# Five more dummy matmuls at the start of a TensorE-bound kernel

## The chip, the cores and the metric

One core of one Trainium2 chip. The metric is device microseconds per execution, the median of several runs; less is better. Each run also lists its span (first to last instruction that the profile shows) and the mean granted clock of TensorE.

## The reference

One transformer block, bfloat16: 2048 rows of 512, modulated layer norm, attention of 32 query heads on 8 key/value heads over the last 512 positions, output projection, then a second modulated layer norm and a ReLU MLP of width 1792.

```
mod = (silu(c) @ w_mod).reshape(1, 6, 1, -1)          # sa, ca, ga, sb, cb, gb
h = layernorm(x) * (1 + ca) + sa
x = x + ga * attention(h, k_cache, v_cache, wq, wo)   # last 512 keys, 32 heads of 128
h = layernorm(x) * (1 + cb) + sb
x = x + gb * (relu(h @ w1) @ w2)
```

## The kernel before

A dummy is a 128x512 product of ones that nobody reads:

```python
def warm(n, gate=(), bk=7):
    for i in range(n):
        mm(bank[bk], ones[:, :], ones[:, 0:1].to_broadcast([P, QB]), True, True, [R_ones] + list(gate), [bk], i == n - 1)
...
    warm(10)                      # from 1.1 us on, while x loads
...
    ln_stat(0)
    warm(3, [R_mv[0]])            # "gated" dummies: behind the statistics of a row tile
    ln_stat(1)
    warm(2, [R_mv[1]])
...
    fs = mod_cols_mm(0, QBK)      # 32 products of one column, in 4 chunks of 8;
    for f in fs:                  # each chunk waits for its own transfer of w_mod
        f()
    ln_tposes(0, TB[0])           # 4 transposes of 128x128
    mod_cols_evac(0, QBK)         # VectorE
...
    ln_tposes(1, TB[0])
    warm(2, bk=1)                 # "the pair"
    ln_norm(2)
    mod_half(0, 0, DVE)           # h = norm * (1 + ca) + sa, from PSUM
    mod_half(0, 2, ACT)
    ln_tposes(2, TB[1])
    ln_tposes(3, TB[1])
    mod_half(0, 1, DVE)
    mod_half(0, 3, ACT)
    q_half(0, 0, CC_ORDER, QBK)   # first query products
```

## Time and profile before

| | before |
|---|---|
| time, median | 560.38 us (560.31 to 560.55) |
| span of the profiled execution | 559.0 us, of 560.87 |
| time beyond the span | 1.9 us |
| TensorE busy | 553.9 us (99%) |

TensorE is the bound from 11.65 us on without a hole (about 0.35 us over the median distances of its shapes in 547 us). The columns are: stretch and length; busy time of TensorE, weight loads, VectorE, ScalarE, GpSimd; mean granted clock; DMA share and GB/s. Before:

```profile
555.00:558.90 3.90, 0.80 (x15) 0.62 (x12) 1.23 (x5) 0.00 (x0) 0.00 (x0) 1.00 0.26 71
558.90:561.00 2.10, 0.00 (x0) 0.00 (x0) 0.00 (x0) 0.00 (x0) 0.00 (x0) 0.72 0.04 12
561.00:564.00 3.00, 0.00 (x0) 0.00 (x0) 0.00 (x0) 0.00 (x0) 0.00 (x0) 0.97 0.00 0
```

No instruction is shown behind 559.0, yet the clock column goes on: the clock's records here say half clock (0.50, from 559.83 us on), and time without a record counts as full (the column reads 1.00 from 0 us on, though the dummies up to 6.56 us start 0.43 us apart and the later ones 0.22). 0.97 over 3 us therefore means that the records stop at about 561.2 (exactly: at 561.17). The execution goes on for some 2 us behind the span.

### The profile page before, as it was taken

The page shows a single profiled execution, that of the slowest core. Times are in us where ns is not written, and L with a number is a line of the kernel's source. Part 1 is how long each engine was busy: PE and PEld are TensorE (multiplying, and loading weights), DVE is VectorE, ACT ScalarE, POOL GpSimd, SP SyncE. Part 2 cuts the span into 40 slices and gives each one's busy share as a digit, 9 for nine tenths or more (in the row PEclk, how much of TensorE's full clock was granted, in tenths as well). Part 3 has the DMA queues.
Part 4 walks back from the last instruction along what each step waited for, and adds up shares of the span by engine and source line. Part 5 has one row for each costly group of instructions (what it writes and reads, how often), then busy time and mean ns, then how long its engine had stood idle before and what let it go on. Part 6 is the DMA issues. An engine that isn't in the chain of part 4 may idle for free.

```text
span 559.0 us, 9759 instructions
## 1 busy us (share of the span) xinstructions
PE 553.9 (99%) x4139; PEld 316.6 (57%) x4139; DVE 254.9 (46%) x556; ACT 349.4 (63%) x455; POOL 52.7 (9%) x50
## 2 busy tenths in 40 slices
PE   8999999999999999999999999999999999999997
PEld 4665555555555555555555555555555554444444
DVE  5555555553546544335445443333354438322134
ACT  5986666666666666666666666666666644432500
POOL 2000022004400000033000000332000000000000
PEclk9999999999999999999999999999999999999999
DMA  9999763422224244353353312121123110200001
GB/s 234 296 196 185 136 166 42 114 43 73 38 41 74 39 84 106 61 130 58 96 95 57 76 40 39 39 38 38 39 39 76 39 29 0 50 28 21 21 29 48
DMA packets 113356, 42.66 MB, mean 76 GB/s; under 512 B 93976, under 2 KB 112152, under 8 KB 113304
## 3 DMA queue, kind: packets, MB, share of 16 engines
q1 hardware_dynamic: 112584, 41.08, 35.5%
q10 hardware_dynamic: 720, 0.89, 0.5%
q8 instruction: 33, 0.54, 0.4%
q14 instruction: 19, 0.16, 0.1%
HBM read 18.35 MB, written 2.10 MB: 37 GB/s over the span
## 4 chain that ended last, share of the span: by engine, by line
PE 98%; DMA 1%; SPq 0%; DVE 0%; issue 0%
PE psS L1374 29%; PE psO L1374 27%; PE psQ L1374 23%; PE psW L1374 20%; DMA wmw<-in_w_mod_dram 1%; SPq L1303 0%; PE psS L1377 0%; PE psO L1377 0%; DVE PT L1752 0%; DVE PT L1754 0%; PE psW L1377 0%
## 5 line engine op out<-in xcount | busy, mean ns | idle before, releaser
L1498 ACT ACTIVATE PT<-psS 128x1024 bf16<-128x1024 f32 x254 | 260.4, 1027 | 127.0 <-PE psS L1374 126.9
L1374 PE MATMUL psS<-qT,kT 128*128 128x512 bf16 (+1 forms) x516 | 151.8, 377 | 0.1
L1374 PEld LDWEIGHTS psO<-v,PT 128*128 128x128 bf16 x2048 | 126.6, 98 | 30.2
L1374 PE MATMUL psO<-v,PT 128*128 128x129 bf16 x2048 | 137.0, 220 | 0.0
L1374 PE MATMUL psW<-wo,oT 128*128 128x512 bf16 x512 | 130.6, 379 | 0.0
L1374 PE MATMUL psQ<-hT,wq 128*128 128x512 bf16 (+1 forms) x508 | 129.6, 377 | 0.0
L1508 DVE RECIPROCAL rinv<-psO 128x4 f32<-128x4 f32 x128 | 23.3, 182 | 225.3 <-PE psO L1374 225.3
L1509 DVE TENSOR_TENSOR o<-psO,rinv 128x512 bf16<-128x512 f32 x128 | 88.5, 691 | 4.7 <-DVE rinv L1508 0.3
L1374 PEld LDWEIGHTS psS<-qT,kT 128*128 128x128 bf16 x516 | 50.0, 98 | 58.7 <-issue 0.4
L1374 PEld LDWEIGHTS psQ<-hT,wq 128*128 128x128 bf16 x508 | 49.7, 98 | 59.0 <-ACT hT L1641 0.2
L1490 ACT ACTIVATE qT<-psQ 128x512 bf16<-128x512 f32 x125 | 73.9, 591 | 0.0
L1741 ACT ACTIVATE wq<-psS 128x512 bf16<-128x512 f32 x56 | 33.4, 597 | 49.1 <-PE psS L1374 49.1
L1374 PEld LDWEIGHTS psW<-wo,oT 128*128 128x128 bf16 x512 | 45.0, 98 | 32.9 <-DVE acc L1531 1.2
L1531 DVE TENSOR_TENSOR acc<-psW,acc 128x512 f32<-128x512 f32 x48 | 33.2, 691 | 6.7 <-PE psW L1374 6.7
L1374 PE MATMUL psO<-wmw,wq 128*128 128x512 bf16 (+1 forms) x168 | 32.9, 352 | 0.0
L1534 POOL TENSOR_TENSOR acc<-acc,gaf 128x512 f32<-128x512 f32 x12 | 15.6, 1301 | 146.9 <-DVE acc L1531 139.8
L1390 POOL TENSOR_TENSOR rstd<-rstd,cst 128x4 f32<-128x4 f32 x7 | 7.2, 1027 | 216.6 <-DVE rstd L1389 216.6
L1752 DVE TENSOR_TENSOR PT<-psO,gbf 128x512 f32<-128x512 f32 (+1 forms) x12 | 7.5, 624 | 40.4 <-PE psO L1374 40.4
L1374 PE MATMUL psS<-h2T,wmw 128*128 128x512 bf16 x112 | 25.3, 379 | 0.0
L1374 PEld LDWEIGHTS psO<-wmw,wq 128*128 128x128 bf16 x168 | 15.4, 98 | 16.5
L1374 PE MATMUL psS<-hT,wmw 128*128 128x512 bf16 x112 | 24.5, 379 | 0.0
L1384 DVE BATCH_NORM_STATS2 st<-x 128x6 f32<-128x512 bf16 x31 | 21.1, 680 | 3.7 <-DMA x<-in_A_x_dram 3.7
(93 smaller groups left out, 197.1 us busy)
## 6 DMA issues: line engine op xcount, KB each, us to landing
wo<-in_A_wo_dram SPq DMA_DIRECT2D x4, 1024.0 KB, 5.9
wq<-in_A_wq_dram SPq DMA_DIRECT2D x7, 512.0 KB, 4.5
wmw<-in_B_w_dram SPq DMA_DIRECT2D x14, 256.0 KB, 3.1
wmw<-in_w_mod_dram SPq DMA_DIRECT2D x4, 512.0 KB, 5.0
oT<-o SPq DMA_TRANSPOSE x128, 2.4
out_dram<-PT SPq DMA_DIRECT2D x15, 128.0 KB, 1.7
x<-in_A_x_dram SPq DMA_DIRECT2D x3, 512.0 KB, 4.3
v<-in_A_v_cache_dram SPq DMA_DIRECT2D x8, 128.0 KB, 4.5
```

The lines of the kernel that those rows point to most:

```text
L1374: kb.op(PE, lambda e: e.matmul(out_ap, lhsT, rhs, start=start, stop=stop), reads=reads, group_writes=[R_b[k] for k in bk], signal=signal)
L1384: kb.op(DVE, lambda e: e.bn_stats(st[:, t, :], x_sb[:, t, :]), reads=[R_x[t]], writes=[R_st[t]])
L1390: kb.op(POOL, lambda e: e.tensor_tensor(rstd[:, sl], rstd[:, sl], cst[:, 0:1].to_broadcast([P, hi - lo]), op=ALU.pow), reads=R_rstd[sl] + ...
L1490: kb.op(ACT, lambda e: e.activation(qT[u % NQT][:, :], bank[bk], ACTF.Copy), reads=[R_b[bk]], writes=[R_qT[u % NQT]])
L1498: kb.op(ACT, lambda e: e.activation(PT[u % NPT][:, pr * 2:pr * 2 + 2, :], s_ps[pr][:, :, :], ACTF.Exp, scale=scale), reads=[R_b[pr * 2], R ...
L1508: kb.op(DVE, lambda e: e.reciprocal(rinv[:, u, :], o_ps[:, :, P]), reads=[R_b[5], R_b[6]], writes=[R_rinv])
L1509: kb.op(DVE, lambda e: e.tensor_tensor(o_sb[u % NOS][:, :, :], o_ps[:, :, 0:P], rinv[:, u, :].unsqueeze(2).to_broadcast([P, TPB, P]), op=A ...
L1531: kb.op(DVE, lambda e: e.tensor_tensor(acc[:, tl, :], bank[WBK], acc[:, tl, :], op=ALU.add), reads=[R_b[WBK], R_acc[tl]], writes=[R_acc[tl]])
L1534: kb.op(eng, lambda e: e.tensor_tensor(acc[:, tl, :], acc[:, tl, :], gaf[:, :], op=ALU.mult), reads=[R_acc[tl], R_ga], writes=[R_acc[tl]])
L1741: kb.op(ACT, lambda e: e.activation(h1T[b % 2][:, fc, :], bank[bk], ACTF.Relu), reads=[R_b[bk]], writes=[R_h1[b % 2][fc]], pre=all_events( ...
L1752: kb.op(DVE, lambda e: e.tensor_tensor(yt[i][:, c0:c1], bank[bk][:, c0:c1], gbf[:, c0:c1], op=ALU.mult), reads=[R_b[bk], R_gb], writes=[R_ ...
```

## The change

The intent is to keep the clock of TensorE up through the thin stretch from 7 to 10 us, where it has only one-column products and transposes.

```diff
     fs = mod_cols_mm(0, QBK)
-    for f in fs:
+    for i, f in enumerate(fs):
         f()
+        if i in (7, 15, 23):
+            warm(1, bk=6)
     ln_tposes(0, TB[0])
...
     ln_tposes(1, TB[0])
-    warm(2, bk=1)
+    warm(3, bk=1)
...
     ln_tposes(3, TB[1])
+    warm(1, bk=1)
     mod_half(0, 1, DVE)
```

## The prediction

> **What bounds the kernel now.** I read the page's engine shares first, then the chain that ended last in order of time, then the TensorE timeline of the first 12 us, the waits of TensorE, and the stretch sums. The page:
>
> ```profile
> PE 553.9 (99%) x4139; PEld 316.6 (57%) x4139; DVE 254.9 (46%) x556; ACT 349.4 (63%) x455; POOL 52.7 (9%) x50
> ...
> PE 98%; DMA 1%; SPq 0%; DVE 0%; issue 0%
> ```
>
> TensorE is busy for 99% of the span and carries 98% of the chain. A busy share alone would not prove it, since matmuls overlap, so I also took every start-to-start distance on TensorE and compared it with the median of its shape (216 ns for 512 columns, 109 for 256, 57 for 129, 56 for 128). Behind 11.65 us the sum of all excess over those medians is about 0.35 us in 547 us: four places near 460 to 474 us with under 0.1 us each. So from 11.65 us on TensorE issues at its own rate, and whatever delays it at the start arrives at the end in full. The chain at the start (start, length, what):
>
> ```profile
> 2.05 6.77 DMA wmw<-in_w_mod_dram
> 8.82 0.05 issue
> 8.87 0.35 PE psQ L1374 x8
> 9.22 0.47 PE psS L1377 x8
> 9.69 0.43 PE psS L1374 x2
> 10.12 0.11 PE psO L1377 x2
> ...
> 10.57 0.52 PE psQ L1374 x4
> 11.09 0.44 PE psO L1374 x4
> 11.52 0.13 issue
> 11.65 0.60 PE psS L1374 x4
> ```
>
> The reader should see that the end is set by the landing of the last of four chunks of the modulation weights at 8.82 us, and by TensorE alone afterwards. The two old dummies (the psS L1374 x2 line at 9.69) are already on that chain with 0.43 us. The TensorE timeline of the same stretch (start, length, instruction, idle before it and what ended that):
>
> ```profile
> 6.56 0.97 PE L1374 MATMUL psW<-ones 128*128 128x512 bf16 x3
> 7.37 0.34 PE L1374 MATMUL psQ<-sc_bf,wmw 128*128 128x1 bf16 x8
> 8.11 0.55 PE L1374 MATMUL psQ<-sc_bf,wmw 128*128 128x1 bf16 x16 [0.40 <-DMA wmw<-in_w_mod_dram]
> 8.87 0.35 PE L1374 MATMUL psQ<-sc_bf,wmw 128*128 128x1 bf16 x8 [0.21 <-DMA wmw<-in_w_mod_dram]
> 9.08 0.61 PE L1377 MATMUL psS<-ident,xn 128*128 128x128 bf16 x8
> 9.53 0.60 PE L1374 MATMUL psS<-ones 128*128 128x512 bf16 x2
> ```
>
> Here TensorE has two holes, before chunk 1 and before chunk 3; chunks 1 and 2 run as one block. In the trace's landings, chunk 2 is complete at 8.24 us, chunk 3 at 8.82.
>
> The purpose of dummies is the clock, so I read that too. The first ten dummies:
>
> ```profile
> 1.10 4.45 PE L1374 MATMUL psW<-ones 128*128 128x512 bf16 x10 [1.10 <-DVE ones L1574]
> ```
>
> (4.45 - 0.63 of the last one) / 9 = 0.42 us from start to start; the pair at 9.53 is 0.60 - 0.38 = 0.22 apart. So the clock doubles in between. The single starts put it among the dummies of 6.56 to 6.94 us, and the trace's clock records hold one entry of full clock, from 6.87 us for 552.96 us, which is past the last matmul. The column of granted clock shows 1.00 from 0 us on, slow dummies included, so it does not separate these two states.
>
> [...]from 7.37 to 9.53 us TensorE has only one-column products, transposes and two holes, and the clock stays full.[...]
>
> **The change part by part.** Nothing is removed. Five 128x512 matmuls of ones are added, only on TensorE: one behind each of the chunks 0, 1 and 2, one more (three for two) between the second and the third transpose group, one behind the fourth. The comparison of instruction order shows no moved instruction and no new wait on any engine. At full clock each takes 216 to 220 ns of TensorE's issue; that is 5 x 0.216 = 1.08 us if nothing is hidden. The starts, step by step:
> - Chunk 0's last product starts at 7.549 and the products are 25 ns apart, so the first dummy runs from 7.574 to 7.79. The next chunk comes at 8.107. Wholly hidden. (Even at half clock, 0.43 us, it would end at 8.00.)
> - Chunk 1: 8 products, 8.107 to 8.297. Second dummy at 8.322. Chunk 2 at 8.322 + 0.218 = 8.540, in place of 8.322; it landed at 8.24, so no other wait. Its last product starts at 8.715.
> - Third dummy at 8.740. Chunk 3 at 8.958, when its data is 0.14 us old. Before it started at 8.868. Behind its wait the first two products were 39 ns apart, without a wait they are 25: the transposes start at 8.958 + 0.200 = 9.158, in place of 9.082. So of 0.65 us of dummies, 0.08 is on the chain.
> - Transposes 0 and 1: 0.443, unchanged (the modulation columns and their DVE evacuation move by the same 0.08). Then three dummies from 9.601 in place of two from 9.525; transposes 2 and 3 start at 10.253, in place of 9.961: +0.29. The DVE tile that they read was done at 9.75, so nothing absorbs this.
> - Their last starts at 10.642, the fifth dummy at 10.697, the first query product at 10.915, in place of 10.405: +0.51.
> - Here a wait returns something. Before, the fourth query product waited for ScalarE's hT: it started at 10.802, 178 ns behind the third, not 109. That hT comes at about 10.75 + 0.08 = 10.83 now, and the fourth product's own turn is 10.915 + 3 x 0.109 = 11.242. The wait is gone: +0.44. The next group starts 109 ns behind it and not 119: +0.43.
> - ScalarE's evacuation of the query, which the score products at 11.65 wait for, follows the fourth product at about 11.55, in place of 11.12. ScalarE is free: its previous tile reads the transposes that now end near 10.81 and takes 0.56, to about 11.41. The score products start at 11.65 + 0.43 = 12.08.
>
> Sum: 0.08 + 0.22 + 0.22 - 0.08 = +0.43 to +0.44 us, all of it before the stretch in which nothing can be won back. 560.38 + 0.43 = 560.8.
>
> **The rivals.** (a) Everything is hidden, 560.4. For it: TensorE does wait 0.40 + 0.21 us in this stretch, by the timeline. Against: the last two dummies stand behind the last of these holes, on a chain that is TensorE all through. (b) Nothing is hidden, 560.38 + 1.08 = 561.5. For it: a 99% busy engine. Against: the first hole is larger than a dummy. (c) The clock. If some executions of the kernel before fell back to half clock[...] the dummies would save it[...]. Against: the profiled execution never falls back, and the three timed ones lie within 0.24 us, which leaves no room for one with and one without. (d) The landing of chunk 3 moves. Later than 8.96 us the first three dummies are free and the sum is 0.36; if it had landed together with chunk 2 they would cost 0.43 and the sum is about 0.8. (e) The delay shifts transfers or evacuations into a better or worse place later. With 0.35 us of stalls in the whole rest there is little to win, and ScalarE with 63% has room to follow.
>
> **Range and chances.** The working gives 0.43; landing times and the returned wait make 0.35 to 0.6 of it; the spread of the runs before is 0.24, and I leave as much for another set of runs. So 560.8, 8 times in 10 between 560.5 and 561.15. Two per cent are 11 us, some ten times the whole cost of the five dummies; only something that none of the views hints at could do that.
>
> **What would show it.** In the profile after: the full-clock record still begins near 6.9 us and never ends early; TensorE's wait before chunk 3 is gone and chunk 3 starts at about 8.96; transposes 2 and 3 start 0.29 later, the first query product 0.51 later, the score products 0.43 later and without a longer wait; the steps behind that are unchanged, so that the last y product shifts by the same 0.43. It would be wrong if the score products stand at 11.65 as before (rival a), if the first three dummies push chunk 3 by more than 0.2 us (chunks landing earlier, or dummies at half clock), or if the clock records of the two kernels differ anywhere behind 12 us.

The 0.43 us of a dummy at half clock is the distance of the first ten in the trace of before (0.426 to 0.427 from the second on).

## More of the kernel before

**Time minus span** will matter; I call it the time beyond the span.

At the end, a flag computed on the chip (are the softmax sums in range?) chooses between finishing and redoing everything with a general version. On TensorE the finishing part comes first and then jumps over the general version:

```python
    kb.emit(stream, e, 0, n_ops)
    e.wait_ge(sems[flag_ev[0]], flag_ev[1])
    v = e.value_load(flag[0:1, 0:1])
    ...
    if name == "pe":
        with e.If(v == 128):
            last_part()           # the last 224 matmuls, then a jump
        with e.Else():
            rerun()               # general version, 5,942 TensorE instructions, never taken here
    # behind both: the barrier in which all engines meet, and the end of the program
```

## The result, and the profile after

| | before | after |
|---|---|---|
| time, median of 6 runs each | 560.35 us (560.02 to 560.66) | 563.04 us (562.88 to 563.56) |
| span of the profiled execution | 559.0 us | 558.9 us |
| span, median of the 6 runs | not listed | 558.9 us |
| time beyond the span | 1.9 us (profiled run) | 4.4 us (median of the 6) |

The ratio is 1.005, interval 1.0037 to 1.0063. (Ratios are the mean time of one kernel's fast runs over that of the other's in the same rounds, so not quite the ratio of these medians.) 2.7 us is six times the predicted 0.43, and far outside the range.

The odd thing is that the profile does not show it: the span did not grow at all. The start after, on TensorE (start, length, instruction):

```profile
7.41 0.38 PE L1374 MATMUL psO<-ones 128*128 128x512 bf16 x1
7.63 0.34 PE L1374 MATMUL psQ<-sc_bf,wmw 128*128 128x1 bf16 x8
7.83 0.38 PE L1374 MATMUL psO<-ones 128*128 128x512 bf16 x1
...
8.46 0.34 PE L1374 MATMUL psQ<-sc_bf,wmw 128*128 128x1 bf16 x8
8.66 0.61 PE L1377 MATMUL psS<-ident,xn 128*128 128x128 bf16 x8
9.32 0.60 PE L1374 MATMUL psS<-ones 128*128 128x512 bf16 x2
9.76 0.27 PE L1377 MATMUL psO<-ident,xn 128*128 128x128 bf16 x2
...
10.42 0.60 PE L1374 MATMUL psQ<-hT,wq 128*128 128x256 bf16 x4
...
11.59 0.60 PE L1374 MATMUL psS<-qT,kT 128*128 128x256 bf16 x4
```

No row has a wait for a transfer: in this execution chunk 3 had landed at 8.22 us, in the one before at 8.82. (Of the three dummies between the transposes two are recorded. The last transpose before them starts at 9.05, so the first dummy's place is 9.11; the two recorded ones start at 9.32 and 9.54.) From the first transpose to the score products it is 11.59 - 8.66 = 2.93 us, before 11.65 - 9.08 = 2.57: +0.36. The prediction has 0.43 - 0.08 = 0.35 for this piece. So the two dummies in this piece do cost what was predicted, and an earlier landing hid it in this one execution. (Score products that stand where they stood before were the prediction's sign for rival (a), that everything is hidden. One trace cannot decide that; the means of e2 and e9 below speak against it.)

The stretch behind the last instruction, after:

```profile
555.00:558.90 3.90, 0.73 (x14) 0.56 (x10) 1.17 (x5) 0.00 (x0) 0.00 (x0) 1.00 0.26 69
558.90:561.00 2.10, 0.00 (x0) 0.00 (x0) 0.00 (x0) 0.00 (x0) 0.00 (x0) 0.67 0.04 8
561.00:564.00 3.00, 0.00 (x0) 0.00 (x0) 0.00 (x0) 0.00 (x0) 0.00 (x0) 0.56 0.01 3
```

0.56 over 3 us is 2 x (1 - 0.56) x 3 = 2.64 us at half clock: the records go on to 563.65, 2.5 us longer than before. That is where the time is. The only other thing in the traces there is the fetching of instructions; TensorE's queue is q8 on the page, and after the change it reads as before:

```profile
q8 instruction: 33, 0.54, 0.4%
q14 instruction: 19, 0.16, 0.1%
```

33 packets of 16,384 bytes. The single records at the end (us from the span's start):

```
                                                   before   after
TensorE's jump at the end of its last part, start  554.65   554.59
  and end                                          558.50   558.25
TensorE's last two block fetches, start            556.17   555.59
                                                   559.27   559.04
last fetch of the other queue (q14), start         560.86   563.12
end of the clock's records                         561.17   563.65
```

In the trace of before, all 34 packets of q8 have 16,384 bytes. From its fetch at 152.0 us to that at 536.8, 22 fetches later, TensorE has run 5,624 recorded instructions, 255.6 to a fetch. So I take q8 for TensorE's queue, and a block for 16,384 bytes or 256 instructions. The jump takes 3.9 and 3.7 us, with one block fetch started inside that time, where the branch at 509.95 us that is not taken takes 0.09. That the jump waits for that fetch was my guess; the traces show the two side by side and no more. Before as after, a further block is fetched at about 559.1, behind the span.

**Theory** (my guess; its mechanism is in no trace). Five matmuls are ten instructions (a weight load and a product each; the page counts 4,144 weight loads against 4,139). They move all code behind them by ten places. By the program, TensorE runs a few more instructions behind the jump and the barrier. If a block border falls among these, TensorE might wait for one more fetch, and the end of the program for TensorE. No profile shows an additional packet: TensorE's queue has the same 34, the one behind the span included, in all seventeen profiles. So the wait could only be for the block at about 559.1, which is fetched in any case. **Rivals:** the dummies themselves cost it, in proportion to their number; or any growth of the program does.

### The profile page after: what moved, and what is told of

The parts are those of the page before. It is cut to its first block, busy times and chain, and to the rows that moved or that the text cites. A ratio compares the mean times of both kernels' runs of the same rounds, so it can differ in the third digit from the quotient of the medians.

```text
span 558.9 us, 9695 instructions
## 1 busy us (share of the span) xinstructions
PE 550.6 (99%) x4070; PEld 317.1 (57%) x4144; DVE 255.0 (46%) x556; ACT 349.7 (63%) x455; POOL 52.7 (9%) x50
## 4 chain that ended last, share of the span: by engine, by line
PE 99%; issue 1%; DVE 0%
PE psS L1374 29%; PE psO L1374 27%; PE psQ L1374 23%; PE psW L1374 20%; PE psS L1377 0%; PE psO L1377 0%; DVE PT L1755 0%; DVE PT L1757 0%; DVE ones L1574 0%; PE psO L1418 0%; PE psW L1377 0%
## 5 line engine op out<-in xcount | busy, mean ns | idle before, releaser
L1374 PE MATMUL psW<-wo,oT 128*128 128x512 bf16 x452 | 118.1, 379 | 3.2
```

The lines of the kernel that those rows point to most:

```text
L1374: kb.op(PE, lambda e: e.matmul(out_ap, lhsT, rhs, start=start, stop=stop), reads=reads, group_writes=[R_b[k] for k in bk], signal=signal)
```

## The experiments

"Shift" is by how many instructions the end of TensorE's program has moved against the kernel before, dummies and padding together. Padding is never executed; it stands at the end of the branch not taken:

```diff
                     gkb.emit(general[name], e)
+                    if name == "pe":
+                        for _ in range(20):              # two waits make one instruction: 10
+                            e.wait_ge(meet, len(fast))   # a constant that holds already
```

The table gives the nominal shift, counted from the waits. When the kernels are built again from their sources, TensorE's program has one instruction more than that wherever padding was added (11 more than before in e1, 257 in e2, 1 in e10 and e14), because the compiler then also puts a jump at the end of that branch. The shifts of 4, 6 and 10 without padding (e3, e4, the changed kernel) are exact, and no conclusion below hangs on the one place.

All fifteen kernels gave the correct result. "Low clock" counts runs whose mean clock was 0.997 or less; span and time beyond it are medians, the span over the other runs. The kernels of one block of rows ran on the same chip, with the runs of before in that block.

| run | what | shift | time, median | span | beyond it | low clock |
|---|---|---|---|---|---|---|
| (before) | | 0 | 560.35 | 558.45 | 1.8 | 3 of 11 |
| e1 | before, padding only | 10 | 562.56 | 558.4 | 4.2 | 0 of 6 |
| e2 | after | 256 | 560.67 | 558.85 | 1.8 | 0 of 6 |
| e3 | chunk dummies only | 6 | 561.38 | 558.5 | 2.9 | 0 of 6 |
| e4 | other two dummies only | 4 | 561.53 | 558.7 | 2.8 | 0 of 6 |
| (before) | | 0 | 560.20 | 558.5 | 1.8 | 0 of 7 |
| e5 | before, padding only | 32 | 560.17 | 558.3 | 1.9 | 0 of 4 |
| e6 | before, padding only | 64 | 560.30 | 558.4 | 1.8 | 1 of 4 |
| e7 | before, padding only | 128 | 560.23 | 558.4 | 1.8 | 0 of 4 |
| e8 | before, padding only | 192 | 560.32 | 558.4 | 1.85 | 1 of 4 |
| (before) | | 0 | 560.31 | 558.4 | 1.8 | 1 of 9 |
| e9 | after | 42 | 560.73 | 558.9 | 1.8 | 0 of 5 |
| e10 | before without the pair | 0 | 559.91 | 558.1 | 1.8 | 0 of 5 |
| e11 | after, 7 dummies between the transposes | 256 | 561.50 | 559.6 | 1.8 | 0 of 5 |
| e12 | before, padding only | 20 | 560.46 | 558.5 | 1.8 | 1 of 4 |
| (before) | | 0 | 560.26 | 558.4 | 1.9 | 0 of 11 |
| e13 | chunk dummies, no pair, nothing behind | 256 | 560.16 | 558.3 | 1.85 | 0 of 5 |
| e14 | before, 2 of the 5 gated dummies | 0 | 561.95 | 558.3 | 1.8 | 5 of 6 |
| e15 | e14 and the chunk dummies | 0 | 561.00 | 558.4 | 1.8 | 3 of 6 |

### The end of the program: e1 to e4

**e1**, the kernel before with the padding above.

> The kernel before with ten more TensorE instructions (semaphore waits) in the branch that is never taken, at its end. Nothing that is executed changes; only the place of the code behind it moves by ten instructions, as in the changed kernel. Fetch theory (the 2.7 us come from where TensorE's last instructions lie relative to its 16 KB instruction blocks): 562.9 to 563.1 us, with a span of 559.0 as before, so that time minus span is about 4.3 and not 1.9. Rival (the five dummies cost the time, by the clock or by their own length): 560.35, as before.

562.56 us with a span of 558.4: 2.2 us longer without one changed instruction in what is executed. Ratio 1.0033, interval 1.0017 to 1.0048; three of the eleven runs of before in it are low-clock ones, so it is rather too small. Its stretches behind the last instruction:

```profile
558.35:561.00 2.65, 0.00 (x0) 0.00 (x0) 0.00 (x0) 0.00 (x0) 0.00 (x0) 0.53 0.02 6
561.00:564.00 3.00, 0.00 (x0) 0.00 (x0) 0.00 (x0) 0.00 (x0) 0.00 (x0) 0.73 0.01 3
```

As after the change, the records run on, here to 562.6. It is a little under the expected 562.9: 0.5 us less than the changed kernel, all of it in the span (558.4 against 558.9), where this kernel has no new dummies.

**e2**, the changed kernel with 246 padding instructions.

> The changed kernel with 246 more never-executed TensorE instructions at the same place, so that with its own ten the code behind has moved by 256 instructions, one whole 16 KB block. Fetch theory: the 2.7 us vanish, 560.3 to 560.9 us; what is left over 560.35 is what the dummies themselves cost (0.43 by the prediction). Rival (the dummies cost it): 563.0, as the changed kernel.

560.67 us, 1.8 beyond the span. One whole block of shift takes the extra 2.6 us beyond the span (4.4 - 1.8) away again, with every dummy still there. Behind its last instruction:

```profile
558.90:561.00 2.10, 0.00 (x0) 0.00 (x0) 0.00 (x0) 0.00 (x0) 0.00 (x0) 0.50 0.04 12
561.00:564.00 3.00, 0.00 (x0) 0.00 (x0) 0.00 (x0) 0.00 (x0) 0.00 (x0) 0.99 0.00 0
```

So e1 and e2 together give the cause of the extra time beyond the span to the place of the code, and both rivals fall: the dummies are in e2 without it, and e2 is the larger program.

**e3** and **e4**, each one part of the change. Against the changed kernel, e3 and then e4:

```diff
-    warm(3, bk=1)
+    warm(2, bk=1)
...
-    warm(1, bk=1)
```

```diff
-        if i in (7, 15, 23):
-            warm(1, bk=6)
```

> Only the three dummies between the chunks (six more TensorE instructions). Fetch theory: one of two levels and nothing between, about 560.4 or about 563.0, depending on which side of a block border six instructions leave the end. Rival (each dummy costs its share): 3/5 of 2.7, 562.0; by the prediction's own sum without the fetch: 560.45.

> Only the third dummy between the transposes and the one behind them (four more TensorE instructions). Fetch theory: one of two levels, about 560.7 or about 563.0; if e3 is at the low level, this one too, since it moves the end by less. Rival (each dummy costs its share): 2/5 of 2.7, 561.4; by the prediction's own sum without the fetch: 560.7.

561.38 and 561.53 us. Here I was wrong: not two levels but one in between, 2.8 to 2.9 us beyond the span, and e4's runs are spread over 2.2 to 3.1. The shift of 4 and that of 6 cost the same, so it is not proportional either. It fits a border that falls behind different instructions of a short tail, some of which have other things to wait for meanwhile, but that is only argued. The traces do show that the delay sits elsewhere. In e3 the last fetch of the other instruction queue (q14) starts 1.47 us behind TensorE's last, much as before (1.59), and the clock's records go on for 1.55 us behind it (before: 0.31). After the whole change it is the other way round: 4.08 us, then 0.53.

### How wide the bad place is: e5 to e8, e12

Padding of 32, 64, 128, 192 and 20 on the kernel before, the same edit.

> The kernel before with 32 never-executed TensorE instructions at the end of the branch not taken. So far the time beyond the span was 1.8 us at a shift of 0 and of 256, 2.8 at 4 and 6, 4.2 to 4.4 at 10. Fetch theory: the border of a block lies inside the few instructions that TensorE executes behind the jump; at 32 it lies earlier in them or ahead of them. If inside, time minus span is 4.2 or more (562.6 or more); if those instructions are fewer than 32 and lie wholly behind the border, it is at most 1.8 (560.3 or less). Rival (any shift of the code costs in proportion): over 5 us beyond the span.

> The same with 64. Fetch theory: 4.2 us or more beyond the span while the border is inside the executed tail, at most 1.8 once it is ahead of the tail. Rival (in proportion to the shift): much over 5 us.

> The same with 128. Fetch theory: as for 64, with more chance of the low level; at most 1.8 us beyond the span and about 560.3 or less. Rival (in proportion): the highest so far.

> The same with 192, 64 short of the whole block. Fetch theory: 1.8 us beyond the span or less, since the border can be reached only from the side of 256. If this one is clearly below 1.8, the kernel before itself pays part of the price, and a shifted one beats it.

> The kernel before with 20 never-executed TensorE instructions, between 10 (4.2 us beyond the span) and 32 (1.9). Fetch theory: 4.2 us or a little more if the border is still behind the jump's target, 562.6 to 563.5; 1.8 if the executed tail is shorter than 20 instructions. It tells how many of the 256 places are bad.

All of them have 1.8 to 1.9 us beyond the span. So shifts of 4, 6 and 10 are bad and 0, 20, 32, 42, 64, 128, 192 and 256 are not: the bad places found lie in one gap of fewer than 20, and the changed kernel hit one. That they come back every 256 places was not tried; a shift of 266 would show it. And 64, 128, 192 and 256 are all multiples of 64, so these runs cannot tell a gap in every 256 places from one in every 64. The kernel before does not pay anything that a shift would save. "In proportion to the shift" is refuted. What e6, e8 and e12 show in their slow runs belongs to the clock, below.

### What the dummies cost themselves: e9, e11, e10

**e9**, the changed kernel with 32 padding instructions, and **e11**, with four more dummies and 238 padding instructions:

```diff
-    warm(3, bk=1)
+    warm(7, bk=1)
```

> The changed kernel with 32 never-executed TensorE instructions at the end of the branch not taken: a shift of 42 in all, where the kernel before (shifts 32 to 192) was back at the low level. Fetch theory: 1.8 us beyond the span; span 0.4 over that of before, 560.6 to 560.7. Clock theory (the dummies keep the clock up): none of its runs has a clock under 0.998, while some of the runs of before and of the kernels without dummies do (so far 5 of 46, each with a span 1.4 to 2.0 us longer). Rival (the fallback is chance of the chip and has nothing to do with the dummies): runs at 0.997 here too.

> The changed kernel with seven dummies in place of three between the transposes, eight more instructions, padded to a shift of 256. Sum of the prediction: 4 x 0.216 = 0.86 us more than the padded changed kernel (560.67), 561.5, all of it in the span, with 1.8 us beyond it. Rival (dummies between the transposes are hidden beside the transfers or the normalisation): 560.7.

Against the full-clock runs of before on the same chip, mean span: e2 558.87 - 558.50 = +0.37, e9 558.82 - 558.49 = +0.33. The prediction's sum was 0.43. Four more dummies between the transposes: e11 559.64 - 558.82 (e9) = +0.82, where 4 x 0.216 = 0.86 was expected. Nothing there is hidden. The parts: e3 +0.0 (predicted 0.08), e4 558.78 - 558.50 = +0.28 (predicted 0.35). Means of 5 to 8 runs whose spans are spread over 0.6 us leave about 0.1 us of doubt on each.

**e10**, the kernel before without its own pair, and four padding instructions:

```diff
     ln_tposes(1, TB[0])
-    warm(2, bk=1)
```

> The kernel before without its own two dummies between the transposes, with four never-executed instructions, so that the shift is 0 and nothing else moves. Sum of the prediction: two dummies of 0.216 us leave the chain, part of it returned by ScalarE's wait: span 0.15 to 0.43 shorter in runs with full clock, 559.9 to 560.2. Clock theory: less TensorE work in the window between 7 and 10 us, so that more of its runs fall back (clock 0.997, about 561.7): at least a third, against about a ninth. Rival (the fallback has nothing to do with dummies): the same rate as before.

559.91 us, span 0.35 us shorter: as expected. But none of its five runs fell to the low clock, where I had expected a third. Five runs are few: at a rate of a third, none in five comes about one time in eight. Counted in stretches of 3.41 us (an estimate from e12 and e15, explained below), the first full-clock stretch in its own trace went from 4.76 to 8.17 us and ended before the pair's place, so by that count the pair did not matter there; in the trace of before, the stretch from 6.87 to 10.28 has the pair in it. So how much the pair does for the clock stays open.

### The clock: e12's trace, e14, e15, e13

Seven of 75 runs without dummies between the chunks (all five gated dummies present) have a mean clock of 0.997 and a span 1.4 to 2.1 us over that of their neighbours; they are the slow runs in the blocks above. The profile of e12 caught one. Its span and clock, then three stretches:

```profile
core 0: 560.4 us, clock 0.997
```

```profile
5.40:8.80 3.40, 2.55 (x32) 1.17 (x32) 3.09 (x12) 2.12 (x9) 2.04 (x4) 1.00 1.40 244
8.81:12.21 3.40, 3.18 (x29) 2.66 (x31) 1.65 (x6) 1.65 (x4) 0.00 (x0) 0.50 1.00 239
12.23:15.60 3.37, 3.24 (x26) 2.31 (x25) 1.71 (x6) 1.96 (x5) 0.00 (x0) 1.00 1.15 321
```

Full clock from 5.39 us, half clock from 8.81 to 12.22, full again: the half-clock stretch is 3.41 us long, the one before it as long to 0.01. On TensorE:

```profile
7.10 0.35 PE L1374 MATMUL psQ<-sc_bf,wmw 128*128 128x1 bf16 x8
8.08 1.07 PE L1374 MATMUL psQ<-sc_bf,wmw 128*128 128x1 bf16 x24 [0.63 <-DMA wmw<-in_w_mod_dram]
9.01 1.01 PE L1377 MATMUL psS<-ident,xn 128*128 128x128 bf16 x8
...
11.52 0.95 PE L1374 MATMUL psQ<-hT,wq 128*128 128x256 bf16 x4
...
13.04 0.27 PE L1374 MATMUL psS<-qT,kT 128*128 128x256 bf16 x1
```

The eight transposes take 1.01 us, not 0.61, and the score products come at 13.04, not 11.65. Note the first stretch: TensorE is "busy" 2.55 of 3.40 us in it and falls back all the same. Busy time counts a one-column product as 0.16 us (163 ns in the trace of before, where they start 25 ns apart). Counted by streamed columns (0.216 us for each 512, the distance of their starts at full clock), the stretch from 5.39 held five dummies, 1.08 us, and no transposes. In the other traces the first full-clock stretch, which begins between 3.8 and 6.95 us, differs: it starts at another place in each. Where the record of full clock runs on, I count it in stretches of 3.41 us from its start. That is an estimate from e12 and e15, where the clock changed after 3.41 us or twice that; it fits that the record of full clock is equally long before and after, 552.959 us, though it begins at 6.87 us in the one and at 6.65 in the other. A stretch was followed by half clock with 0.65 us (e14), 1.08 (e12) and 1.1 to 1.2 (e15, where one dummy straddles the start); it was not with 1.23 (e5), 1.29 (e10) and more (all others, of which the kernel before has 0.87 of dummies and products and 0.74 of transposes). So for these traces I estimate, from the values just listed, a limit of about 1.2 of 3.41 us, if transposes count like products. Whether they do is not shown: without its transposes the kernel before has 0.87, less than the 1.08 of e12, and it stayed up. Either they count, or the limit is not one of streamed columns. That is read from stretches at full clock; the way back up comes under e15.

**e14**, the kernel before with two of its five gated dummies and six padding instructions:

```diff
     ln_stat(0)
-    warm(3, [R_mv[0]])
+    warm(1, [R_mv[0]])
     ln_stat(1)
-    warm(2, [R_mv[1]])
+    warm(1, [R_mv[1]])
```

> The kernel before with two in place of five dummies behind the layer-norm statistics (6 to 7 us), six never-executed instructions, shift 0. Clock theory (a stretch of 3.41 us with under about 1.15 us of streamed columns, transposes counted, is followed by half clock): stretches that begin between about 4.9 and 6.2 us are now poor, that is some 1.3 of 3.4 us of possible beginnings, so about 4 in 10 runs at 0.997 and 561.5 or more; the others at 560.3. Rival (chance of about one in ten, whatever TensorE does there): none or one run of six.

The 3.41 us is the stretch of e12, the 1.15 lies between its 1.08 and the 1.23 of e5, and the 4 in 10 is an estimate that takes all beginnings within a stretch as equally likely.

Five of six runs at low clock, two of them at 0.993 and 0.994, median 561.95. More than the 4 in 10 expected, but far from one in ten (and from the 0 of 11 of before on that chip): with less TensorE work there, the rate is higher, and the stretch begins elsewhere from one execution to the next (3.8 to 6.95 us in the other traces).

**e15**, the same, with the first hunk of the change (the three dummies between the chunks) and no padding:

```diff
     for i, f in enumerate(fs):
         f()
+        if i in (7, 15, 23):
+            warm(1, bk=6)
```

> The same two in place of five, and three dummies put between the chunks: as many dummies as before, 0.65 us of them moved into the waits for the transfers. Shift 0. Clock theory: back to a stretch as full as in the kernel before or fuller, so none or one run of six at 0.997, the rest at about 560.4. Rival (the place of the dummies right behind the statistics is what counts): as e14.

Three of six. I had expected none or one: as many dummies, but later. Its trace shows why. The full-clock stretch began at 4.32 and ended at 7.73, before the second of the moved dummies:

```profile
4.32:7.72 3.40, 2.22 (x22) 0.91 (x20) 2.83 (x10) 2.06 (x8) 1.04 (x2) 1.00 1.19 318
7.74:11.14 3.40, 3.04 (x35) 1.83 (x33) 1.93 (x8) 1.30 (x3) 0.99 (x3) 0.50 1.09 182
11.15:14.55 3.40, 3.40 (x21) 2.55 (x20) 1.28 (x4) 1.91 (x6) 0.00 (x0) 0.50 1.16 313
```

Half clock for two stretches. The second of them held the pair and two of the moved dummies, some 3,010 columns with the transposes, and was still followed by half clock; e12's half-clock stretch held at least 3,400 and was followed by full. At full clock e5 stayed up with some 2,950 (its 1.23 us). Whether climbing back needs more columns than staying up, these cases lie too close to tell. In this trace the two moved dummies behind 7.73 us did nothing for the stretch that ended there; and where a stretch begins differed from trace to trace (3.8 to 6.95 us).

**e13**, the changed kernel with the three between the chunks alone, and 254 padding instructions:

```diff
     ln_tposes(1, TB[0])
-    warm(3, bk=1)
...
     ln_tposes(3, TB[1])
-    warm(1, bk=1)
```

> Only the three dummies between the chunks; none between the transposes (not even the two of before) and none behind; 254 never-executed instructions make the shift 256. From e3 (chunk dummies alone add about 0.05 us to the span) and e10 (the pair costs 0.35): span 558.1 to 558.2, 1.8 beyond it, 559.9 to 560.0: faster than before and than the changed kernel. Clock theory: no run under 0.998. Rival (the dummies between the transposes are needed for the clock): some runs at 0.997 and 561.5.

560.16 us, no low clock in five runs. Not clearly faster than before: mean span 558.40 against 558.46 for the eleven runs of before on that chip, all at full clock; ratio 0.9997, interval 0.9984 to 1.001. So the 0.35 of e10 and the 0.0 of e3 do not simply add; why is not shown. Without the pair the third transpose group waits for VectorE's normalised tile, but by as much in e10 (0.30 us) as here (0.29). The score products come at 11.12 us here and at 11.27 in e10; what the profiled run of e13 loses against that of e10, it loses behind them (547.5 us from there to the end of the span against 547.1). In all, 0 of 33 runs with dummies between the chunks and the five gated ones fell to the low clock (after itself, e2, e3, e9, e11, e13), against 7 of 75 without. At 7 in 75, 33 clean runs would come by chance about one time in 25 (one in 14 if one asks how often seven low runs, drawn at random from all 108, would all fall among the 75); together with the traces I take the protection as likely, not as proved by the counts alone.

## Why the prediction was wrong

- **The step that failed** is the last line of the sum, "560.38 + 0.43 = 560.8": it adds a change of the span to a time, and so takes the time beyond the span for a constant. It was 1.9 us before and 4.4 after. The same error stands in "The comparison of instruction order shows no moved instruction": none moved in order, but everything behind moved by ten places, and no rival asked what lies behind the jump. e1 shows the missing 2.2 to 2.5 us with no dummy at all, and e2 shows the dummies without it.
- **The dummies' own cost was right in size**: 0.43 predicted, 0.33 to 0.37 measured (e9, e2), of it 0.28 for the two around the transposes and about 0 for those between the chunks. With the end out of the way the changed kernel takes 560.67 to 560.73, inside the predicted range. No experiment took the returned wait of ScalarE's tile by itself; the trace after has the four query products 0.109 us apart, as that step says.
- **The landing of chunk 3** was taken from one profile, at 8.82 us. In the profiles of the fifteen kernels and of the changed one it lies between 7.53 and 8.85. Rival (d) named this; I gave it too little room. "TensorE's wait before chunk 3" is, in eight of the ten profiles without dummies between the chunks, a wait of the transposes for the normalised rows instead (e1: last product at 8.06, first transpose at 8.60), and the dummies lie in it just as well.
- **Rival (c), the clock, was put aside wrongly.** "The three timed ones lie within 0.24 us, which leaves no room for one with and one without": three runs are too few for something that happens about one time in eleven. What it would cost is now measured: the low-clock runs are 1.4 to 2.1 us longer; 3.41 us at half clock, as in e12, would make 3.41 / 2 = 1.7, an estimate. The dummies' benefit there is likely but small on the average: 7/75 x 1.7 = 0.16 us, an estimate from these counts, against a cost of 0.35, so on the average the padded changed kernel should still be the slower one, by some 0.2 us. (Its median is slower by 0.3 to 0.4 us, but a median leaves rare slow runs out.)

What stays open: the few TensorE instructions behind the barrier are not in the trace, so which of them stands behind the block border, and why a shift of 4 or 6 costs 1.0 us and one of 10 costs 2.4 to 2.6, is inferred from the shifts alone. That the place of the code costs the time is shown (e1, e2); that it does so by the wait for a fetch is an explanation, not something seen. A count on the kernel before, built again, fits it: from 150 us to the jump, TensorE's fetches start when the instruction being executed stands 158 to 192 places into a block of 256, counted from the program's start, and the jump's target stands at 188. Which block each fetch brings is not in the traces, so this is support and no proof.

## What to carry to other kernels

Compare time minus span before you explain a difference by the trace: if the span has not moved, look behind the last instruction, and repeat the run with never-executed padding before you credit or blame a small change. An instruction added anywhere ahead of it moves the end of the program; here, behind a jump over a long branch, a move by 4 to 10 instructions cost 1 to 2.6 us, and one by 20 or more nothing. A dummy that is to keep the clock up belongs into the stretch that would otherwise be thin; do not read that from busy time alone (e12 fell to half clock behind a stretch with 2.55 us of busy time and 1.08 us of streamed columns), and judge the need over many runs (7 low ones in 75 here).
